# An attention and MLP kernel under another order table, with 38 products of zeros at its start and its flag behind the last result

## The chip, the cores and the metric

The kernel runs on one core of a Trainium2 chip. The metric is the device time of one execution in microseconds. TensorE (PE; PEld for its weight loads) multiplies, VectorE (DVE) and ScalarE (ACT) work element by element, GpSimd (POOL) does next to nothing here, and SyncE (SP) issues all DMAs, in one queue.

## The reference

Soft-capped attention over 4 batches of 12 heads (448 tokens, 64 columns a head), followed by a two-layer MLP with a sigmoid gate (768 to 2048 to 768). The MLP's weights arrive as 64-bit floats, and `q` and `k` are drawn some 5.8 times larger than 0.1 times a normal variable.

```python
scores = scale * np.matmul(q, k.transpose(0, 1, 3, 2))
scores = cap * np.tanh(scores / cap)
attn = np.exp(scores - np.max(scores, axis=-1, keepdims=True))
attn = attn / (np.sum(attn, axis=-1, keepdims=True) + 1e-09)
x = np.matmul(attn, v)                        # heads side by side: 1792 x 768
h = x @ w_in
out = (h * (1.0 / (1.0 + np.exp(-1.702 * h)))) @ w_out
```

## The kernel before

Heads are handled in pairs: 4 batches of 6 pairs make 24 units. A unit loads `q`, `k` and `v`, multiplies scores into two double banks `s` in four groups (three of two blocks, one of a single block), takes a tanh from each into `t` and an exponential into `p` on ScalarE, sums the exponentials with products by ones into the bank `sm`, and multiplies them with `v` into the single bank `pa`. The first seven units do so in 32-bit floats, with tiles in the room of `wo`; the later ones split every operand into two 16-bit halves (`qh`, `ql`, `vh`, `vl`). Of most units ScalarE copies `sm` to `f` and `pa` to `pu`; the sums go by DMA through memory (`sd`, `rsum`), VectorE takes reciprocals (`rr`), two more DMAs spread them (`rd`, `rb`), and VectorE makes the two halves of `x`. Units 4 and 5 divide directly, without the DMAs.

The MLP's first product takes `x` of all six units of a batch, one after the other, into one of two banks `m`: for each unit a chunk of three products, high by high, high by low, low by high. The weights come in half pieces of 512 KB as pairs of 32-bit words (tiles `g` and `wo`), and VectorE decodes them with integer steps into `wi_h` and `wi_l`; two of the passes can stand on ScalarE instead. The last two batches share seven products in place of eight in banks `z`, with sums of weights made on VectorE.

Every operation is recorded first (`Plan.op`), with a model cost. A table in the source, `ORDER`, then gives the whole order: which operation comes when, on which engine where two could do it, and which buffer of a ring each tile takes. `timed` computes start times by the model's costs and lags, and `emit` writes the instructions in that order; each engine runs its own in order. `keep_busy` would add products of zeros where the model sees TensorE idle before the first `m`; neither kernel has one from it, only those written out ahead. Before the table's first operation VectorE fills constants (lines 411 to 423), ending with the zeros `wz`, and TensorE multiplies zeros 16 times (line 427).

At the end small operations (lines 1253 to 1270) judge whether the ranges allowed the fast path and write one number, `flag`. All engines read it (line 365) and branch (line 366) to the end or into `general_path`, a slower kernel for any input. In the traced run no line of `general_path` was executed.

Of the kernel before, what the change touches and what calls it, by code (L numbers as in the profile page):

```python
# [11 lines left out]
F16 = mybir.dt.float16  # L12
F32 = mybir.dt.float32
# [24 lines left out]
EV_ON = ("AV", "AV")  # L38
SPLIT_ON = "A"
# [12 lines left out]
READ_ACC = 0.083  # L52
PE_COL = 0.0004222
# [3 lines left out]
LAG = {"PE": 0.165, "ACT": 0.1, "DVE": 0.085, "SP": 2.6}  # L57
DMA_ISSUE, DMA_BW = 0.5, 0.36
# [15 lines left out]
    "wI-b@8<=EjnaQR=;GUae%9+}MbtZwSVoI2TW~xbO)|;y4wyR+_m^!9#V7tj@c9^<>BBokkr`cs%nR@1sNn~1^X=b=-6R2*kyZinbrk!bTMwoYIo@r~|n=xjj>0l0<v1X?EU>@j?W}F!nc;tGTUM8{W80c;KnDJ(}"
    "x$g#=zGgz8lNn@YnSN%u8EyKT&Vd1Dc3_41VY--=fsJO4S!m`5ewvBqp#PVdYc`pu=7=e3Hk+enfeA6cO%t=nJa%O7xV>hZd0}pvErIFgmRV)k9x$r|Vh`y>0ne^6&jLOZ#~w6(bK5L7Ndj?gQgh5~HFwPEz`np4"
    "bH%(2+%*9c&pvQh&3&`q6brmE8Et&~z<e?Z>{)ZoB)8AqLzlunHwo?aKuVj%K5@lOD*MpfFpX_4``H9dZu`Q0F?sAc^TeDt$ITK0_N99iIAOk<ljdvSlzD7kxx6-O@Pc{mirA+vG|<F;Gs-5i+7`7-1I`w+iS1k0"
    ")S@-PX7-)S6dY{A*=44=jT}s3qgZQO*w^Nw$!C)W2ia^kwSD7S+Gj4AEpF4;^7fO9YSY^AHnY8FN?5;57mQ$A*@*VD%Wosu^tN?ylr3O0*a|izINC<Dg>7^@#uf}#v_4zXR<fn+SX<d%3beIl?H5<YmJW`yZEOr1"
    "2$r**Y$4m(z6n&dU)^}y&X%#?To?P^0k*e&><1ULU2R|6&Av6Yf<tVFU~L=IX1Cp~!qc{+t!8`J33iI@X{+0zcA~9e`&o^3Y)$*!eRRX@N;}Z*u>FIp>}As{xYG`>!-K2sNNaGHooaX6x^|i!Ve8p7c2e+!U2CTY"
    "Ev~aOt;0QbvR!XC+Z@3S_J`YRx7b<sknL^v**NaHJrkT^>)Y9Oqup;W+O2khJ!@~+h4zw-?{3<h_GIvujb%gaZHsu=zObk4w%|*<$TqNd>`%AdzOqN`YrDx_wr}il`_>)^-n9?yFE_{Dvk5}y+QpV|iG641+1U1I"
    "aK61}#a#&=vz}uN=ib{#HoRMEui6j62=1}9E*#zuKC^>^5uJ0-ZEE+xMsp2=EnIkv8~WRQvIlJ%_aqo*(Is`??MM5=rgap$%$~F9+*8}yC3ERrLYKiscb{!M7s-9GKW%as*=2R?Vz{sNn~i{tY#x`<#da}6tGFnk"  # L80
    "nOt5M%jI+V-7lNXMZ^N`w-t<p1zjpv(-m^HT#C@luCS}^vb&V7jyoR&*U{w&&E@L4mZ5E2Jr^0Px=t>OYwTj+R#(mCbUR#US0ps5^RSD{?Yg=Pwu$TQVq*2sZmy^+=9H`N!dw*W?uxsnE*3U$C0yyy9<EtvNms_z"
    "aHU)#7aIq-s2B&QyJ$GjHFwc*hKq}>+)P*24RL+kEEf+4xrU+fF~s$CjofUv+-?hP>*hG0o9p~;p4;HcxqwUT%Dcpv0Qb3}F6j2VexXTlnd|9>g|4s*-Tctu?tts>D!7gApgZJrXfL<OEq9@Afm`7gyCm+gONb|2"
    "QXK4-geJn3E*Z|oBW{&j>gM5UmmDj)5pIne=|;Ju?xY*-&bqWX#!U!Khnw6)H`c9n?c6wb%58V!-OkXFxY?Z!-Hf~3D4gWd;}+cFGT>+&i)Y+9w-r<1HXMiZaSWb!$J`#A>@wno&?#;bR&p0zAuNn3u?QB$y_gwG"
    "4Nir|mBxKI9#dl`oQ#!S8f+gr4X3&}gFCqWxBw>%K99TI6fA@5LbKphoQO*>D=x+LZaU7z6?g$xVh&t}*>Dvu$FexhmBa0r7oTA<%!!Y&IOfA#SORBYZY+s;up+L-nV22RV<o(Zvv3_=!aZ&W-oU+XC$7iJxO(tS"
    "JnpLCJzRtN@fPkHTos=TzKpwZ16Ic?SO9Nh1uTdM@F3p7LwFdEU=2Jm_$qG1lXw)X;Zr<@_ptyS$7_S@;7@#xZ}0(L#}8N&PvKj9IJhn@#25Gu3)4rui|_Ff*28r43DZ-3{EENuGd942VVS5Fe!<%K8*|e)JdK&D"
# [12 lines left out]
    "|GMSBccA}Mwf{m)4gdG6|999L?ZDW-<$~1?i8a!nvgc3D?~G#g=SQiKft@w%fc}IbD6+)H5nI&oS139(^arfL*}wA1(Vyv`lk>mAe*o)%ulf"
# [49 lines left out]
class Plan:  # L148
# [158 lines left out]
    def timed(self, pre, seqs):  # L307
# [6 lines left out]
        while any(at[e] < len(s) for e, s in seqs.items()):  # L314
            moved = False
            for e, s in seqs.items():
                while at[e] < len(s) and all(start[p] is not None for p, _ in pre[s[at[e]]]):
# [9 lines left out]
                    if e == "SP":  # L327
                        done[i] = pipe = max(pipe, t + us) + o.mb / DMA_BW
# [1114 lines left out]
```

## Time and profile before

| | us |
|---|---|
| runs without a profile, median of 3 (591.09 to 592.51) | 591.7 |
| the profiled execution | 594.05 |
| its span, first to last instruction | 591.9 |
| TensorE busy in the span | 577.8 |
| VectorE busy | 542.0 |
| ScalarE busy | 399.3 |

The profiled execution took 2.15 us more than its span, and 2.35 us more than the median of the runs without a profile. An engine's busy time says how much work it had, not whether anybody waited for it; for that there are the waits (who waited for whom, and how long) and the order of time. Units 0 to 6 end near 84 us; from there on the MLP's products fill TensorE.

### The profile page before, as it was taken

How to read it: one execution, taken by the hardware profiler on the slowest of the kernel's cores; microseconds unless marked ns; L12 is line 12 of the kernel's file. 1: busy time of each engine (PE TensorE's matmuls, PEld its weight loads, DVE VectorE, ACT ScalarE, POOL GpSimd, SP SyncE). 2: the span in 40 equal slices, each digit the busy share in tenths (PEclk: the TensorE clock that was granted, in tenths of full speed). 3: DMA queues.
4: the chain of work that ended last, by engine and by line, in shares of the span. 5: the costliest groups of instructions: out<-in, count | busy, mean ns of one | idle time of the engine just before them, and what ended most of it. 6: DMA issues, size and time to landing. Idle time of an engine off the chain costs nothing.

```text
span 591.9 us, 9836 instructions
## 1 busy us (share of the span) xinstructions
PE 577.8 (98%) x3674; PEld 288.5 (49%) x3674; DVE 542.0 (92%) x904; ACT 399.3 (67%) x617; POOL 0.2 (0%) x4
## 2 busy tenths in 40 slices
PE   7998899999999999999999999999999999999995
PEld 3333345555555554544555555555555555555552
DVE  4998999999999999999999999988999999988932
ACT  5998899989789899898787687434445543421110
POOL 0000000000000000000000000000000000000000
PEclk9999999999999999999999999999999999999999
DMA  8999763624567544343433444312222210000201
GB/s 298 328 239 294 227 239 108 205 71 139 157 172 209 193 141 141 95 137 110 148 86 101 120 153 133 104 48 81 88 71 82 64 45 0 17 0 1 79 31 69
DMA packets 45559, 74.36 MB, mean 126 GB/s; under 512 B 14952, under 2 KB 30912, under 8 KB 45504
## 3 DMA queue, kind: packets, MB, share of 16 engines
q1 hardware_dynamic: 45504, 73.66, 40.2%
q8 instruction: 31, 0.51, 0.3%
q14 instruction: 24, 0.20, 0.1%
HBM read 61.68 MB, written 11.95 MB: 124 GB/s over the span
## 4 chain that ended last, share of the span: by engine, by line
PE 73%; DVE 15%; DMA 5%; issue 3%; ACT 1%; SPq 1%; DVEq 0%
PE m L257 39%; PE z L257 22%; PE s L257 5%; PE pa L257 5%; DVE wo L222 3%; DVE p L222 2%; DMA sd<-f 2%; PE sm L257 2%; DMA g<-in_moe_w_in_dram 1%; DMA rb<-rd 1%; DVE g L222 1%; DVE rb L222 1%; DVE ta L222 1%; DVE ql L222 1%; DVE wi_l L222 1%
## 5 line engine op out<-in xcount | busy, mean ns | idle before, releaser
L257 PE MATMUL m<-g,wo 128*128 128x448 f16 x624 | 126.4, 353 | 0.0
L257 PEld LDWEIGHTS <-wo 128*128 128x128 f16 x864 | 83.4, 98 | 80.5 <-issue 3.6
L214 ACT ACTIVATE t<-s 128x896 f32<-128x896 f32 (+1 forms) x96 | 77.5, 823 | 22.9 <-DVE p L222 12.8
L257 PEld LDWEIGHTS <-wi_h 128*128 128x128 f16 x528 | 50.5, 98 | 53.1 <-issue 7.6
L257 PE MATMUL m<-x,wi_h 128*128 128x448 f16 x234 | 63.6, 353 | 1.4 <-DVE x L222 0.7
L222 DVE TENSOR_TENSOR p<-t,p 128x896 f16<-128x896 f32 (+1 forms) x62 | 58.5, 951 | 0.7 <-ACT p L238 0.4
L257 PE MATMUL m<-xa,wi_h 128*128 128x448 f16 x198 | 53.7, 353 | 0.0
L214 ACT ACTIVATE t<-t 128x896 f32<-128x896 f32 (+1 forms) x62 | 51.9, 846 | 0.6
L238 ACT ACTIVATE p<-t 128x896 f16<-128x896 f32 (+1 forms) x54 | 45.1, 841 | 3.3 <-PE pa L257 3.0
L257 PE MATMUL s<-qh,kk 128*128 128x448 f16 (+3 forms) x152 | 46.0, 377 | 0.0
L222 DVE SCALAR_TENSOR_TENSOR wo<-wo 128x1024 int32<-128x1024 int32 (+2 forms) x42 | 44.3, 1065 | 0.2 <-ACT wo L238 0.2
L257 PE MATMUL s<-ql,kk 128*128 128x448 f16 (+1 forms) x136 | 42.0, 353 | 0.0
L257 PE MATMUL m<-x,wi_l 128*128 128x448 f16 x117 | 41.2, 353 | 0.0
L257 PEld LDWEIGHTS <-stg 128*128 128x128 f16 x288 | 28.2, 98 | 26.3
L257 PEld LDWEIGHTS <-wi_l 128*128 128x128 f16 x264 | 25.8, 98 | 25.0 <-issue 1.0
L257 PE MATMUL pa<-p,vh 128*64 128x448 f16 x272 | 37.5, 355 | 0.2 <-DVE rb L222 0.2
L257 PE MATMUL m<-xa,wi_l 128*128 128x448 f16 x99 | 34.9, 353 | 0.0
L257 PEld LDWEIGHTS <-kk 128*128 128x128 f16 (+1 forms) x272 | 23.3, 101 | 22.5 <-issue 2.7
L257 PEld LDWEIGHTS <-xa 128*128 128x128 f16 x216 | 21.0, 98 | 19.6
L238 ACT ACTIVATE xa<-x 128x1024 f16<-128x1024 f32 x9 | 9.4, 1055 | 30.1 <-PE z L257 15.0
L257 PE MATMUL s<-wo 64*128 64x448 f32 (+1 forms) x96 | 24.7, 622 | 3.4 <-DMA wo<-in_q_dram 1.8
L257 PE MATMUL sm<-p,ones 128*32 128x224 f16 (+2 forms) x544 | 26.5, 306 | 0.0
(278 smaller groups left out, 1092.8 us busy)
## 6 DMA issues: line engine op xcount, KB each, us to landing
wo<-in_moe_w_in_dram SPq DMA_DIRECT2D x18, 512.0 KB, 5.4
stg<-in_kx_dram SPq DMA_DIRECT2D x17, 448.0 KB, 4.3
stg<-in_qx_dram SPq DMA_DIRECT2D x17, 448.0 KB, 3.8
stg<-in_moe_w_out_dram SPq DMA_DIRECT2D x16, 384.0 KB, 5.8
wo<-in_moe_w_out_dram SPq DMA_DIRECT2D x16, 384.0 KB, 8.4
sum<-xa SPq DMA_DIRECT2D x32, 192.0 KB, 3.7
stg<-sum SPq DMA_DIRECT2D x32, 192.0 KB, 2.9
rb<-rd SPq DMA_DIRECT2D x44, 112.0 KB, 3.2
```

What stands on the lines that cost most here:

```text
L214: self.nc.scalar.activation(real(out), real(in_), func, scale=real(scale), **b)
L222: getattr(self.nc.vector, name)(out=real(out), **{k: real(x) for k, x in ins.items()}, **kw, **a)
L238: self.nc.scalar.activation(real(out), real(in_), AF.Copy, scale=1.0 if f is None else f, **b)
L257: self.nc.tensor.matmul(real(o), real(w), real(x), start=a, stop=z)
```

## The change

The table `ORDER` is another one, made with a larger lag of DMAs (2.9 in place of 2.6 us, and 0.5 us more before 80 us), of ScalarE and VectorE, and with a cost for VectorE's operations that begin in the upper half of the partitions. The zeros are filled first, TensorE multiplies 38 of them (zeros by zeros, no ones), and the flag is written behind the last result. `general_path` becomes two loops over 48 heads and over 64 parts of the MLP, with an own copy `vn` of `v`; before, it was a loop over 24 units, a decoding that was written out, and a loop over 4 batches.

```diff
-LAG = {"PE": 0.165, "ACT": 0.1, "DVE": 0.085, "SP": 2.6}
-DMA_ISSUE, DMA_BW = 0.5, 0.36
+LAG = {"PE": 0.165, "ACT": 0.109, "DVE": 0.087, "SP": 2.9}
+DMA_ISSUE, DMA_BW, DMA_EARLY = 0.5, 0.36, 0.5
+WARM = 38
+UPPER = 0.23
...
 ORDER = (
-    "c-p;p1F+{!vSpSMzqW1Lwr$(C-F^SKecQHe+qP}nHeY`;`(|f1Uc`%;c)L|~PE}-NMpd1tjHpxqU_gTf1Of;7z2p!LQiBI6AUX)7fou>LQbGjC1u-Bkq=J}`6e2=)U`PiAy-1K7VnG?m0g)jORDjqJ1<FDk$O{!A"
+    "c-p;}bFe4RlIXLP=&^0vwr$(CJ#)S|bH=u9+qP}nHg|sa?!LXT`yzJt#=cis`RUAz?5M7+%0F5G0D=Y!1_&HPgVc~5(m)Ex1rZ=3q=ak`2_i#UNCinDI(QHTazlEE3If@o0wjSLkO$&IOvnLcAQmvBgR&40@<K(("
...
+        if any(isinstance(x, Ref) and x._at(0).base_partition() for x in w + list(ins.values())):
+            us += UPPER
...
                         done[i] = pipe = max(pipe, t + us) + o.mb / DMA_BW
+                        done[i] += DMA_EARLY * (t < 80.0)
...
-        r = tc.nc.values_load(flag, min_val=0, max_val=1)
+        r = tc.nc.values_load(flag)
         with tc.If(r > 0):
-            general_path(tc, q, k, v, cap, w_in, w_out, out)
+            general_path(tc, q, k, vn, cap, w_in, w_out, out)
...
+    wz = sb.tile([P, 128], F16, name="wz")
+    nc.vector.memset(wz, 0.0)
     capt = sb.tile([P, 1], F32, name="capt")
...
-    wz = sb.tile([P, 128], F16, name="wz")
-    nc.vector.memset(wz, 0.0)
     ps_m = ring([P, 512], F32, "m", 2, ps)
     plan.zeros, plan.idle_bank = wz, ps_m
-    for _ in range(16):
-        nc.tensor.matmul(ps_m["tiles"][0][:32, :128], ones16[2], wz, start=True, stop=True)
+    for _ in range(WARM):
+        nc.tensor.matmul(ps_m["tiles"][0][:32, :128], wz[:, :32], wz, start=True, stop=True)
...
-        with tc.For_i(0, B * NP) as u:
+    with tc.tile_pool(name="g_att", bufs=1) as att, tc.For_i(0, N) as i:
...
-    with tc.tile_pool(name="g_mlp", bufs=1) as mlp, tc.For_i(0, B) as b:
+    with tc.tile_pool(name="g_mlp", bufs=1) as mlp, tc.For_i(0, NFC * B) as i:
...
+    host["vn"] = inputs["v"].reshape(B * H, S, D)
```

Three places of the order. The first is SP's queue where the last `k` and `q` of batch 0, those of unit 5, are loaded (`wo<-in_k`, `wo<-in_q`); `in_moe_w_in` are half pieces of `w_in`, `sd`, `rsum`, `rd` and `rb` the sums on their way through memory, `kk` belongs to unit 6. Before:

```order
L263 DMA sd_156<-f_146 4x224
L263 DMA wo<-in_k_dram 128x448
L263 DMA wo<-in_moe_w_in_dram 128x1024 x2
L263 DMA rsum<-sd_156 112x2x4
L263 DMA kk_130<-in_k_dram 128x448
L263 DMA wo<-in_q_dram 128x448
L263 DMA sd_157<-f_144 4x224
```

Now, in the same queue:

```order
L267 DMA wo<-in_moe_w_in_dram 128x1024 x2
L267 DMA wo<-in_k_dram 128x448
L267 DMA rsum<-sd_179 112x2x4
L267 DMA rd_180<-rr_176 112x2x4
L267 DMA wo<-in_q_dram 128x448 x2
L267 DMA wo<-in_k_dram 128x448
L267 DMA sd_178<-f_168 4x224
```

The last `q` stood behind 18 half pieces of `w_in`; it now stands behind 14, next to the `q` of unit 4.

The second place is TensorE between the first chunks of the MLP (`m<-x`, two banks) and the chunks of the next unit's `x`. `sm` and `pa` are those of units 4 and 5, `s<-qh,kk` the scores of unit 6. Before, from the second chunk's last product on:

```order
L257 MATMUL m_91<-x,wi_l 128x448
L257 MATMUL sm_160<-p_142,ones_2_74 64x448 x2
L257 MATMUL sm_160<-p_143,ones_0_72 64x448
L257 MATMUL sm_160<-p_143,ones_1_73 64x448
L257 MATMUL pa_161<-p_140,wo 64x448 x2
L257 MATMUL s_165<-wo 128x448 x2
L257 MATMUL pa_161<-p_141,wo 64x448 x2
L257 MATMUL pa_161<-p_142,wo 64x448 x2
L257 MATMUL sm_160<-p_139,ones_2_74 64x448 x2
L257 MATMUL pa_161<-p_143,wo 64x448 x2
L257 MATMUL s_165<-qh_132,kk_130 128x448 x2
L257 MATMUL s_166<-wo 64x448 x2
```

There the third chunk follows. Now, the rows just ahead of the third chunk:

```order
L261 MATMUL sm_182<-p_162,ones_2_76 64x448 x2
L261 MATMUL sm_182<-p_163,ones_2_76 64x448 x2
L261 MATMUL sm_182<-p_164,ones_0_74 64x448
L261 MATMUL sm_182<-p_164,ones_1_75 64x448
L261 MATMUL pa_183<-p_161,wo 64x448 x2
L261 MATMUL pa_183<-p_162,wo 64x448 x2
L261 MATMUL pa_183<-p_163,wo 64x448 x2
L261 MATMUL pa_183<-p_164,wo 64x448 x2
L261 MATMUL s_188<-qh_155,kk_152 64x448 x2
L261 MATMUL s_187<-qh_155,kk_152 128x448 x2
L261 LDWEIGHTS wi_h
L261 MATMUL m_90<-x,wi_h 128x448
```

All of unit 5's sums and products with `v` and all scores of unit 6 now come ahead of the third chunk; before, they came behind the fifth, except for one group of unit 6's scores and one of unit 5's sums.

The third place is VectorE's end: `z` and `m` are banks with the last products, `cnt` and `flag` the verdict. Before:

```order
L1269 TENSOR_REDUCE cnt<-cnt 1x1
L222 SCALAR_TENSOR_TENSOR f_146<-m_90,stg_128 128x448
L1270 TENSOR_SCALAR flag<-cnt 1x1
L222 SCALAR_TENSOR_TENSOR rb_148<-m_91,stg_128 128x448
L222 SCALAR_TENSOR_TENSOR f_145<-z_4009,stg_129 128x448
L365 TENSOR_LOAD flag
```

Now:

```order
L1274 TENSOR_REDUCE cnt<-cnt 1x1
L224 SCALAR_TENSOR_TENSOR f_168<-m_90,stg_150 128x448
L224 SCALAR_TENSOR_TENSOR stg_148<-m_91,stg_150 128x448
L224 SCALAR_TENSOR_TENSOR rb_169<-m_91,rb_169 128x448
L224 SCALAR_TENSOR_TENSOR stg_149<-z_4018,rb_169 128x448
L1275 TENSOR_SCALAR flag<-cnt 1x1
L370 TENSOR_LOAD flag
```

The flag went from ahead of the last two results to behind the last one; SP's read of it went from between its stores to behind the last store.

## Rows read from the trace of the kernel before

**Rows 1.** The page's busy times: us, share of the span, instructions.

```profile
PE 577.8 (98%) x3674; PEld 288.5 (49%) x3674; DVE 542.0 (92%) x904; ACT 399.3 (67%) x617; POOL 0.2 (0%) x4
```

**Rows 2.** Stretches: us, busy of each engine (instructions), granted clock, DMA share, GB/s.

```profile
0.00:10.00 10.00, 6.75 (x30) 3.69 (x32) 1.76 (x22) 3.89 (x5) 0.20 (x4) 1.00 0.73 244
10.00:40.00 30.00, 29.65 (x230) 10.71 (x234) 29.38 (x39) 29.85 (x42) 0.00 (x0) 1.00 0.97 324
40.00:64.00 24.00, 20.12 (x106) 6.75 (x98) 20.18 (x27) 20.05 (x27) 0.00 (x0) 1.00 0.94 252
84.00:245.00 161.00, 160.80 (x1105) 83.24 (x1102) 158.83 (x268) 146.73 (x226) 0.00 (x0) 1.00 0.49 148
```

**Rows 3.** TensorE's waits: who waited for whom, us in total, times, longest.

```profile
PE s L257 <- DMA wo<-in_q_dram: 1.8, 1, 1.8
PE pa L257 <- ACT pu L238: 0.7, 1, 0.7
PE m L257 <- DVE x L222: 0.7, 1, 0.7
PE m L257 <- ACT x L238: 0.7, 1, 0.7
```

**Rows 4.** TensorE in order of time: start, us, operation, count [idle before <- releaser].

```profile
1.92 1.86 PE L427 MATMUL m<-wz,ones 128*32 128x128 f16 x16 [1.92 <-DVE thr L1253]
5.12 5.77 PE L257 MATMUL s<-wo 64*128 64x448 f32 x16 [1.34 <-DMA wo<-in_k_dram]
12.61 1.77 PE L257 MATMUL s<-wo 64*128 64x448 f32 x8
19.47 1.02 PE L257 MATMUL s<-wo 64*128 64x448 f32 x4
49.64 1.77 PE L257 MATMUL s<-wo 64*128 64x448 f32 x8 [1.75 <-DMA wo<-in_q_dram]
```

**Rows 5.** ScalarE in order of time, 7 to 21 us.

```profile
7.02 0.92 ACT L214 ACTIVATE t<-s 128x896 f32<-128x896 f32 x1 [4.78 <-PE s L257]
8.51 0.92 ACT L214 ACTIVATE t<-s 128x896 f32<-128x896 f32 x1 [0.58 <-PE s L257]
20.00 1.24 ACT L238 ACTIVATE wo<-wo 128x1024 f32<-128x1024 f32 x1
```

**Rows 6.** VectorE in order of time, 0 to 78 us.

```profile
0.82 0.06 DVE L411 MEMSET warm<- 128x1 f32 x1 [0.82 <-PEq L1416]
18.00 0.69 DVE L222 TENSOR_SCALAR wo<-wo 128x1024 int32<-128x1024 int32 x1
18.72 1.25 DVE L222 SCALAR_TENSOR_TENSOR wo<-wo 128x1024 int32<-128x1024 int32 x1
77.31 0.62 DVE L222 SCALAR_TENSOR_TENSOR x<-rb,x 128x448 f16<-128x448 f32 x1
```

**Rows 7.** VectorE's waits until 84 us: the row of w_in's pieces.

```profile
DVE wo L222 <- DMA wo<-in_moe_w_in_dram: 2.4, 2, 2.0
```

**Rows 8.** SP's queue in order of time, 27 to 43 us.

```profile
27.26 0.81 SPq L263 DMA_DIRECT2D wo<-in_moe_w_in_dram  x2
42.88 0.42 SPq L263 DMA_DIRECT2D wo<-in_q_dram  x1
```

**Rows 9.** The end in order of time: last result and last store.

```profile
585.65 0.62 DVE L222 SCALAR_TENSOR_TENSOR f<-z,stg 128x448 f32<-128x448 f32 x1 [1.07 <-PE z L257]
586.39 0.40 SPq L263 DMA_DIRECT2D out_dram<-f  x1
```

**Rows 10.** Lines 365 and 366: count, ns min/median/max, first and last start.

```profile
L365 PEldq TENSOR_LOAD <-flag x1: 488/488/488, 584.1 to 584.1; - x1
L366 SPq EVENT_SEMAPHORE  x8: 17/17/17, 587.4 to 590.6; - x8
L366 ACTq COMPARE_BRANCH  x1: 45/45/45, 584.4 to 584.4; - x1
L366 PEldq COMPARE_BRANCH  x1: 4227/4227/4227, 584.7 to 584.7; - x1
```

More of the change, by code (lines that the diff above doesn't have):

```diff
@@ L99 @@
+    "|9I>F8Cs(q82i^D8><}>YotFvJO-@$(<};^6l(idl6ID?Vzi13X>g<s8q0s)Lx(_4BmCt!{6qTl_{Zk_zv;gKl?<^8"
 )
@@ L357, in keep_busy, with tile_kernel @@
             self.nc.tensor.matmul(out[:cols, :128], z[:rows, :cols], z[:rows], start=True, stop=True)
-def tile_kernel(tc, q, k, qx, kx, v, cap, w_in, w_out, out):
+def tile_kernel(tc, q, k, qx, kx, v, vn, cap, w_in, w_out, out):
     with ExitStack() as outer:
@@ L1290, in general_path @@
     P = 128
-    NC = 7
-    NV = 8
+    N = B * NP * 2
+    QC = 112
+    NQ = S // QC
     NCC = DM // P
     NFC = DFF // P
-    QC = 112
-    NQ = S // QC
+    assert B == 4
+    M = DM * DFF // (N * P)
     drm = ctx.enter_context(tc.tile_pool(name="g_drm", bufs=1, space=bass.MemoryType.DRAM))
-    xt = drm.tile([B * NP, P, S], F32, name="xt")
-    md = drm.tile([2, S], F32, name="md")
+    xt = drm.tile([N, D, S], F32, name="xt")
+    md = drm.tile([1, S], F32, name="md")
+    wd = drm.tile([2, N, P, M], F32, name="wd")
     cst = ctx.enter_context(tc.tile_pool(name="g_cst", bufs=1))
-    ones = cst.tile([P, D], F32, name="ones")
-    nc.vector.memset(ones, 1.0)
     capt = cst.tile([P, 1], F32, name="capt")
@@ L1406 @@
-_INS = ["q", "k", "qx", "kx", "v", "cap", "moe_w_in", "moe_w_out"]
+    acc = cst.tile([P, B, NCC, S], F32, name="acc")
+    nc.vector.memset(acc, 0.0)
+    ps = ctx.enter_context(tc.tile_pool(name="g_ps", bufs=1, space=bass.MemoryType.PSUM))
+    qf, kf = (a.rearrange("b p (j d) s -> (b p j) d s", j=2) for a in (q, k))
+    bits = [w.bitcast(I32).rearrange("r n -> (r n)").rearrange("(i p m) -> i p m", p=P, m=2 * M) for w in (w_in, w_out)]
+    with tc.tile_pool(name="g_att", bufs=1) as att, tc.For_i(0, N) as i:
+        kd = att.tile([D, S], F32, name="kd")
+        qd = att.tile([D, S], F32, name="qd")
+        vo = att.tile([QC, NQ, 2 * D], F32, name="vo")
+        st = att.tile([P, 2, M, 2], I32, name="st")
+        one = bass.ds(i, 1)
+        nc.sync.dma_start(kd, kf[one].rearrange("o r s -> (o r) s"))
+        nc.sync.dma_start(qd, qf[one].rearrange("o r s -> (o r) s"))
+        nc.sync.dma_start(vo[:, :, :D], v[one].rearrange("o (c p) d -> (o p) c d", p=QC))
+        nc.vector.memset(vo[:, :, D:], 1.0)
+        for w in range(2):
+            nc.sync.dma_start(st[:, w].rearrange("p m t -> p (m t)"), bits[w][one].rearrange("o p m -> (o p) m"))
+        af = att.tile([P, 2, M], F32, name="af")
+        a = af.bitcast(I32)
+        L, H = st[:, :, :, 0], st[:, :, :, 1]
+        nc.vector.tensor_single_scalar(out=a, in_=H, scalar=0x7FFFFFFF, op=ALU.bitwise_and)
+        nc.vector.tensor_scalar(out=af, in0=af, scalar1=2.0**-15, scalar2=122880.0, op0=ALU.max, op1=ALU.min)
+        nc.vector.tensor_scalar(out=a, in0=a, scalar1=0x38000000, scalar2=3, op0=ALU.bitwise_xor, op1=ALU.logical_shift_left)
+        nc.vector.tensor_single_scalar(out=a, in_=a, scalar=0x7FFFFFFF, op=ALU.bitwise_and)
+        nc.vector.scalar_tensor_tensor(out=a, in0=L, scalar=29, in1=a, op0=ALU.logical_shift_right, op1=ALU.bitwise_or)
+        nc.vector.scalar_tensor_tensor(out=a, in0=H, scalar=-(2**31), in1=a, op0=ALU.bitwise_and, op1=ALU.bitwise_or)
+        nc.sync.dma_start(wd[:, one].rearrange("w o p m -> (o p) w m"), af)
+        qk = ps.tile([P, NCC, 512], F32, tag="s", name="qk")
+        for c in range(NQ):
+            nc.tensor.matmul(qk[:QC, c, :S], qd[:, c * QC:(c + 1) * QC], kd, start=True, stop=True)
+        mx = att.tile([QC, NQ], F32, name="mx")
+        nc.vector.tensor_reduce(out=mx, in_=qk[:QC, :NQ, :S], op=ALU.max, axis=AX.X)
+        nc.sync.dma_start(md.rearrange("o (c p) -> (o p) c", p=QC), mx)
+        mb = att.tile([QC, 1, S], F32, name="mb")
+        nc.sync.dma_start(mb[:, 0], md.to_broadcast([QC, S]))
+        nc.scalar.activation(mb, mb, AF.Tanh, scale=tsc[:QC])
+        kq = ps.tile([P, NCC, 512], F32, tag="s", name="kq")
+        for c in range(NQ):
+            nc.tensor.matmul(kq[:QC, c, :S], kd[:, c * QC:(c + 1) * QC], qd, start=True, stop=True)
+        t = att.tile([QC, NQ, S], F32, name="t")
+        nc.scalar.activation(t, kq[:QC, :NQ, :S], AF.Tanh, scale=tsc[:QC])
+        nc.vector.tensor_tensor(out=t, in0=t, in1=mb.to_broadcast([QC, NQ, S]), op=ALU.subtract)
+        nc.scalar.activation(t, t, AF.Exp, scale=capt[:QC])
+        pa = ps.tile([P, 512], F32, tag="pa", name="pa")
+        for c in range(NQ):
+            nc.tensor.matmul(pa[:, :S], vo[:, c], t[:, c], start=(c == 0), stop=(c == NQ - 1))
+        r = att.tile([D, S], F32, name="r")
+        nc.vector.tensor_scalar_add(r, pa[D:, :S], 1e-9)
+        nc.vector.reciprocal(out=r, in_=r)
+        nc.vector.tensor_tensor(out=r, in0=pa[:D, :S], in1=r, op=ALU.mult)
+        nc.sync.dma_start(xt[one].rearrange("o r s -> (o r) s"), r)
@@ new lines, in general_path @@
+    xv = xt.rearrange("(b c j) d s -> b (j d) c s", b=B, j=2)
+    wiv = wd[0].rearrange("i p m -> (i p m)").rearrange("(c p f n) -> f p c n", c=NCC, p=P, f=NFC)
+    wov = wd[1].rearrange("i p m -> (i p m)").rearrange("(f p n) -> f p n", f=NFC, p=P)
+    with tc.tile_pool(name="g_mlp", bufs=1) as mlp, tc.For_i(0, NFC * B) as i:
+        f = bass.ds(nc.s_assert_within(i >> 2, 0, NFC - 1, skip_runtime_bounds_check_because="i < 4 * NFC"), 1)
+        b = bass.ds(nc.s_assert_within(i & 3, 0, B - 1, skip_runtime_bounds_check_because="two bits"), 1)
+        x = mlp.tile([P, NCC, S], F32, name="x")
+        wi = mlp.tile([P, NCC, P], F32, name="wi")
+        wo = mlp.tile([P, DM], F32, name="wo")
+        nc.sync.dma_start(x, xv[b].rearrange("o p c s -> (o p) c s"))
+        nc.sync.dma_start(wi, wiv[f].rearrange("o p c n -> (o p) c n"))
+        nc.sync.dma_start(wo, wov[f].rearrange("o p n -> (o p) n"))
+        hp = ps.tile([P, 512], F32, tag="pa", name="hp")
+        for c in range(NCC):
+            nc.tensor.matmul(hp[:, :S], wi[:, c], x[:, c], start=(c == 0), stop=(c == NCC - 1))
+        e = mlp.tile([P, S], F32, name="e")
+        nc.scalar.activation(e, hp[:, :S], AF.Exp, scale=-1.702)
+        nc.vector.tensor_scalar_add(e, e, 1.0)
+        nc.vector.reciprocal(out=e, in_=e)
+        nc.vector.tensor_tensor(out=e, in0=hp[:, :S], in1=e, op=ALU.mult)
+        op = ps.tile([P, NCC, 512], F32, tag="s", name="op")
+        for d in range(NCC):
+            nc.tensor.matmul(op[:, d, :S], wo[:, d * P:(d + 1) * P], e, start=True, stop=True)
+        mine = acc[:, b].rearrange("p o c s -> p (o c) s")
+        nc.vector.tensor_tensor(out=mine, in0=mine, in1=op[:, :, :S], op=ALU.add)
@@ L1409 @@
+    for b in range(B):
+        nc.sync.dma_start(out.rearrange("(d p) (b s) -> b p d s", p=P, s=S)[b], acc[:, b])
+_INS = ["q", "k", "qx", "kx", "v", "vn", "cap", "moe_w_in", "moe_w_out"]
 def kernel(**inputs):
```

161 lines of the change are left out of this document (35 added, 126 removed).

## The prediction

> **What bounds the kernel now.** The busy shares come first [rows 1]: TensorE is busy for 577.8 of 591.9 us, VectorE for 542.0, ScalarE for 399.3. An order of instructions cannot take work from TensorE, only holes, so the second view is the stretches [rows 2]: between 40 and 64 us TensorE is busy for 20.12 of 24, later it is without holes (160.80 of 161 from 84 us). The third view says which holes count [rows 3]: one wait of 1.8 us for a q that was loaded late, 0.7 us for ScalarE to empty the bank of `pa`, and twice 0.7 us for x, all between 41 and 64 us. The last view is the start in order of time [rows 4, 5]: after 16 products of zeros TensorE idles 1.34 us until q and k of the first pair are there at 5.12, and its first 16 rows of `s` take 5.77 us, while 8 rows of the same kind take 1.77 us at 12.61. That is half the rate: zeros of 128 columns at one in 0.116 us on average, and `s` at 0.36 against 0.22 us a row, part of it waiting. The column of the granted clock reads 1.00 there [rows 2], so the lower of the two levels (1.2 against 2.4 GHz) is seen in the durations alone. Everything before 64 us that becomes earlier on TensorE can move the end; later there is next to nothing to win, but VectorE is nearly full from 84 to 245 us (158.83 of 161) and can take a lead back.
>
> **The general path** was not run: the flag was 0, and no row of the trace has one of its lines. Its new loops count only as code that the last branch jumps over (below). The two new planner terms and the lags count only through the table made with them.
>
> **Term 1, the start.** The memset of the zeros moves from last to first on VectorE, which begins at 0.82 [rows 6], so the products can start near 0.95 instead of 1.92. Thirty-eight at 1.86 / 16 = 0.116 us take 4.4 us at most and end at 5.4 at the latest, 0.3 us behind the landing at 5.12; the 1.86 us holds the last one's way through the array, so near 5.1 is likelier. TensorE then has no hole before the first `s`. Before, the first `s` was slow from 5.12 for some 4 us; with work since 0.95 the faster level should come near the first `s`. Upper bound of the gain: a block of four rows takes 1.02 us at the later rate [rows 4], so ScalarE's first tanh starts at 5.12 + 1.02 + 0.04 = 6.18 and not 7.02; the second block is ready at 5.12 + 1.77 = 6.89, its tanh follows the first at 7.02 instead of 8.51 [rows 5], and the exponentials start 1.5 us earlier. Lower bound: the level comes as late as before, or the zeros overrun, -0.3. I take 1.3 us of gain, near the upper end, since one block may still be slow. Between 10 and 40 us TensorE, VectorE and ScalarE are busy for 29.65, 29.38 and 29.85 of 30 us, so a lead at 10 us is kept if no engine gets more to do there. By the order, ScalarE has less: 10 instead of 14 decoding passes of 1024 columns (1.24 us each) up to the last exponential of the seventh pair. VectorE gets four of them at 0.69 us, but three integer steps of 1.25 us fall behind the last x of batch 0 [rows 6]: 2.8 - 3.8, so it reaches that x about 1 us of work sooner.
> By the Trainium skill (TensorE: Matmul & The Clock Gate, section Part 1: The HAM clock gate) the number of slow products at a kernel's start differs from run to run, as the moment of the rise is not tied to the first product. By it this term would be anything between its two bounds, and no run here yet shows which.
>
> **Term 2, the waits between 41 and 64 us.** They sum to 1.8 + 0.7 + 0.7 + 0.7 = 3.9 us [rows 3]. The q of the sixth pair was issued at 42.88 [rows 8], behind 18 half pieces of w_in, and the products that need it start at 49.64 [rows 4]. In the new order of SP's queue it stands behind 14; the 14th left at 27.26 to 28.1. Even if it goes five us after that, it lands before 41: the 1.8 us go. The second chunk of h waited twice 0.7 us for x of the second and third pair; in the new order all remaining products of the sixth pair and three `s` blocks of the seventh stand between the first chunk and the second: 1.4 us go. The 0.7 us behind `pu` stay: the bank is still single and `pu` still stands behind a decoding pass on ScalarE. What is late next: w_in's pieces, which give way to q and k on the queue, so waits of VectorE for w_in and of TensorE behind it. The nearest rows are VectorE's longest wait for w_in, 2.0 us [rows 7], and TensorE's own waits of 0.7 to 1.8 us. I put one new wait at 1.4 us, between these. Sum: -1.8 - 1.4 + 1.4 = -1.8 us; bounds -3.9 (all go, none comes) and +1.8 (none goes, one like the longest comes).
>
> **Term 3, from 64 to 585 us**: 0. Counts of each kind of work on each engine differ by a handful of passes, about +0.5 us on VectorE over the whole kernel, and TensorE's changes between kinds of products are 128 instead of 130. Bounds: 0 to +2.2, VectorE's idle time of 161 - 158.83 us, which is what it can still catch up if it comes late.
>
> **Term 4, the end.** Before, the flag was written ahead of the last two results; SP read it between the last stores, and TensorE at 584.1. Now every engine reads it behind the last result (before at 585.65 + 0.62 = 586.27 [rows 9]). SP loses the stop for the read between the stores, but the last store is gated by the last result anyway, at 586.39, and SP's waits for landings end at 590.6 [rows 10]. TensorE's read took 0.49 us and its branch 4.23, ScalarE's branch 0.05. If that stays, TensorE is through at 586.27 + 0.2 (an estimate for the flag) + 0.5 + 4.3 = 591.3, behind SP's last landing and ahead of the span's end at 591.9, which comes after SP's checks of all queues. I take +0.1; bounds -0.4 (stores less crowded) and +0.5.
> The Trainium skill (Runtime: NRT & Kernel Launch, section Instruction fetch mechanics) says that a taken branch to code outside what is held has to fetch it first. By that, the shorter general path would make TensorE's branch cheap and this term 0 or below; the 4.23 us agree that such a fetch exists.
>
> **Sum**: -1.3 - 1.8 + 0 + 0.1 = -3.0 us. The profiled execution took 594.05 us, 2.15 more than its span of 591.9; with the change such a one would take 591.05. The runs without a profile have a median of 591.7, 2.35 below the profiled one, and the same step gives 588.7 us.
>
> **Rivals.**
> Given back at VectorE: TensorE leads by 3 us at 64 us, but between 84 and 245 us VectorE is busy for 158.83 of 161 us, and TensorE runs into it. For: 2.2 idle us in 161 are little to catch up with. Against: VectorE's own waits before 64 us fall away too, 24 - 20.18 = 3.8 us in the stretch from 40. If only 0.5 us survive: 591.2.
> The clock comes no earlier, since TensorE's zeros use 32 of its columns: term 1 is 0, -1.8 + 0.1: 590.0. For: the 16 zeros of before did not bring it. Against: they were followed by 1.34 us of nothing.
> Everything goes: -1.5 - 3.9 - 0.4 = -5.8: 585.9. For: this is all that the waits hold. Against: static orders seldom lose all waits without a new one.
> Slower: VectorE starves for w_in. Four half pieces slip behind q and k, and if its waits for w_in grow from 2.4 to over 5 us, its work of 84 to 245 us starts late by more than the idle 2.2 us there, and TensorE waits for it: +2.2 us, 593.9. For: the 2.4 us [rows 7] are this very wait, and DMA is full there (share 0.94). Against: three integer steps of decoding were put off in the same order. It decides from the point at which VectorE's last x of batch 0 is later than 77.31 + 0.6 = 77.9 us, where it is now [rows 6].
>
> **Chances.** Forecast 0.48, with its own range 586.5 to 590.5 (term 1 from -0.6 to -1.5, term 2 from -0.7 to -3.3, the end from +0.1 to -0.4, rounded); given back 0.17; clock no earlier 0.08; everything goes 0.10; slower 0.17. About 0.2% (1.2 us) is what a measurement of this kernel can tell from no change. Faster: 0.48 + 0.10 + half of the clock's case, which lies 0.29% off, 0.04 = 0.62; within: 0.17 + 0.04 = 0.21; slower 0.17. The range goes from 585.0 to 593.5: it leaves out a half of the starved case and of the largest gain.
>
> **What would show it.** The first tanh at 6.2 to 6.6 and the second `s` block at the later rate (term 1); no wait of `s` for q, and fewer than 3 us of holes on TensorE between 41 and 64 (term 2); TensorE busy for 160 of 161 us in the stretch that answers to 84 to 245 (term 3); from TensorE's last product to the end of the span 6.3 us as now, and TensorE's branch as the only late engine (term 4). I am wrong if the tanh starts at 7 us, or if TensorE's lead at the end of batch 0 is there and is gone at 245 us, or if VectorE's waits for w_in grow.

## The result, and the profile after

The changed kernel takes 586.28 us (median of 4 runs, 585.83 to 587.47); the kernel before, run beside it, takes 592.11 us (591.09 to 592.58). The ratio is 0.9909, with an interval of 0.9893 to 0.9925: 5.8 us less by the medians, where 3.0 were forecast. The profiled execution took 586.16 us with a span of 584.1, against 594.05 and 591.9; that execution of before lay about 2 us above its median, so the spans differ by more than the medians do.

The busy times, as in [rows 1] (us, share of the span, instructions):

```profile
PE 577.9 (99%) x3696; PEld 289.4 (50%) x3696; DVE 542.1 (93%) x902; ACT 401.0 (69%) x619; POOL 0.2 (0%) x4
```

The work is the same to 0.1 us on TensorE and VectorE. The stretches, as in [rows 2] (busy of PE, PEld, DVE, ACT, POOL):

```profile
0.00:10.00 10.00, 8.72 (x56) 5.64 (x57) 3.07 (x19) 4.34 (x6) 0.20 (x4) 1.00 0.74 241
10.00:40.00 30.00, 30.00 (x240) 11.34 (x240) 29.75 (x44) 29.71 (x41) 0.00 (x0) 1.00 1.00 343
40.00:64.00 24.00, 23.12 (x116) 7.86 (x114) 23.96 (x30) 23.07 (x32) 0.00 (x0) 1.00 0.91 273
84.00:245.00 161.00, 161.00 (x1105) 82.93 (x1103) 158.69 (x267) 144.83 (x224) 0.00 (x0) 1.00 0.47 144
```

The third row is the one that moved: TensorE is busy for 23.12 of 24 us in place of 20.12, and VectorE for 23.96 in place of 20.18. TensorE's waits up to 90 us, as in [rows 3]:

```profile
PE m L432 <- DVE warm L418: 1.0, 1, 1.0
PE pa L261 <- ACT pu L242: 0.8, 1, 0.8
PE s L261 <- ACT t L216: 0.3, 1, 0.3
```

The waits for q and for x are gone, the one for `pu` is there as before. VectorE's wait of 2.4 us for pieces of `w_in` in `wo` [rows 7] has no row any more; for pieces in `g` it waits 3.7 us, all of it before 8.1 us. TensorE and then ScalarE in order of time, as in [rows 4, 5]:

```profile
1.00 4.24 PE L432 MATMUL m<-wz 128*32 128x128 f16 x38 [1.00 <-DVE warm L418]
5.26 2.57 PE L261 MATMUL s<-wo 64*128 64x448 f32 x8
8.09 1.92 PE L261 MATMUL s<-wo 64*64 64x448 f32 x8 [0.25 <-ACT t L216]
9.94 0.97 PE L261 MATMUL pa<-p,wo 128*64 128x448 f32 x4
```

```profile
7.12 1.73 ACT L216 ACTIVATE t<-s 128x896 f32<-128x896 f32 x2 [4.88 <-PE s L261]
```

The zeros end at 5.24 without a hole behind them, yet the first eight rows of `s` still take 2.57 us, against 1.77 at the later rate, and the first tanh starts at 7.12, not at 6.2 to 6.6. The second eight rows are at the later rate, and the first product of `pa` is at 9.94.

The end, VectorE's last result and SP's last store, as in [rows 9]:

```profile
580.09 0.62 DVE L224 SCALAR_TENSOR_TENSOR stg<-z,rb 128x448 f32<-128x448 f32 x1 [0.91 <-PE z L261]
```

```profile
580.74 0.33 SPq L267 DMA_DIRECT2D out_dram<-stg  x1
```

The last result begins 5.56 us earlier (585.65 - 580.09). From there to the end of the span it was 591.9 - 585.65 = 6.25 us and is now 584.1 - 580.09 = 4.0. In these last microseconds every engine reads the flag and branches, and SP waits until its stores have landed, as in [rows 10] (count, ns min/median/max, first and last start):

```profile
L371 SPq EVENT_SEMAPHORE  x8: 17/17/17, 582.2 to 582.8; - x8
L371 PEldq COMPARE_BRANCH  x1: 236/236/236, 581.4 to 581.4; - x1
L371 DVEq COMPARE_BRANCH  x1: 72/72/72, 581.4 to 581.4; - x1
L371 DVEq EVENT_SEMAPHORE  x1: 21/21/21, 582.0 to 582.0; - x1
```

TensorE's branch takes 0.24 us in place of 4.23. VectorE's, of 0.07 us, is followed by its next event after 0.6 us. In the kernel before that gap was 3.8 us, which the branch row alone does not show:

```profile
L366 DVEq COMPARE_BRANCH  x1: 72/72/72, 586.5 to 586.5; - x1
...
L366 DVEq EVENT_SEMAPHORE  x1: 21/21/21, 590.3 to 590.3; - x1
```

The last events of the kernel before are this one, at 590.3 us, and SP's, at 590.6 [rows 10], which wait for the last stores. Both are early now; which of them held the end cannot be read from these rows.

### The profile page after: what moved, and what is told of

The parts are those of the page before. It is cut to its first block, busy times and chain, and to the rows that moved or that the text cites. A ratio compares the mean times of both kernels' runs of the same rounds, so it can differ in the third digit from the quotient of the medians.

```text
span 584.1 us, 9864 instructions
## 1 busy us (share of the span) xinstructions
PE 577.9 (99%) x3696; PEld 289.4 (50%) x3696; DVE 542.1 (93%) x902; ACT 401.0 (69%) x619; POOL 0.2 (0%) x4
## 4 chain that ended last, share of the span: by engine, by line
PE 90%; DVE 6%; DMA 2%; ACT 1%; issue 1%; SPq 0%; ACTq 0%; DVEq 0%
PE m L261 48%; PE z L261 22%; PE s L261 9%; PE pa L261 8%; PE sm L261 3%; DVE wo L224 2%; DVE g L224 2%; DVE wi_l L224 1%; DMA g<-in_moe_w_in_dram 1%; DMA rb<-rd 1%; DVE wi_h L249 1%; SPq L267 0%; ACT p L216 0%; DVE g L249 0%; ACT wo L242 0%
## 5 line engine op out<-in xcount | busy, mean ns | idle before, releaser
L216 ACT ACTIVATE t<-s 128x896 f32<-128x896 f32 (+1 forms) x96 | 77.9, 821 | 17.1 <-PE s L261 8.5
L261 PE MATMUL pa<-p,vl 128*64 128x448 f16 x136 | 24.2, 352 | 0.0
```

Of the source, the lines that this page charges most:

```text
L216: self.nc.scalar.activation(real(out), real(in_), func, scale=real(scale), **b)
L261: self.nc.tensor.matmul(real(o), real(w), real(x), start=a, stop=z)
```

## The experiments

Theory: the table, the start and the general path each give a share, and the shares add up. Rivals: that one part carries the lead, or that a part works only with another. Each kernel ran beside the kernel before; ratios are against it, and intervals are in brackets.

**One part alone, and one part undone.** `table_only`, `start_only` and `general_only` put one of the diff's three parts into the kernel before. `no_general`, `no_start` and `no_table` are the changed kernel with one part as it was.

```diff
 # table_only: ORDER, LAG, DMA_EARLY, UPPER of the changed kernel
 # start_only
+    wz = sb.tile([P, 128], F16, name="wz")      # ahead of the constants
...
-    for _ in range(16):
+    for _ in range(38):
...
 # general_only: the new general_path, and
-        r = tc.nc.values_load(flag, min_val=0, max_val=1)
+        r = tc.nc.values_load(flag)
```

> The kernel before with the new order table alone (and the costs it was made with, and the flag behind the last result that comes with it); old start of 16 products, old general path. Theory A (the lead comes from the table's placing of work before 80 us, 4.7 us of the 5.6 us that TensorE leads by at its last product; the other 0.9 us come from the start): TensorE's last product ends 4.7 us earlier than before's; time -4.7 us, about 587.4, if the end costs what it cost before, and 588 to 589 if the branch of some 4 us now stands behind the last result and ends last. Rival B (the start is what carries the lead, by the clock, and the table fits only a kernel that started early): under 2 us of gain, 590.5 to 592.

> The kernel before with the new start alone (zeros filled first, 38 products of zeros); old table, old general path. Theory A: the later groups of the first scores are quicker, TensorE is ahead by 0.9 us at 10 us, but the old table's waits between 41 and 64 us for a late q and for w_in's pieces stand where DMA puts them, so at most 0.9 us reach the end: 591.2 to 592.1. Rival B: 3 us or more of gain, under 589.5.

> The kernel before with the new general path alone (not executed, since the flag is 0); old table, old start. Theory A (the time from TensorE's last product to the end of the span falls from 6.3 us, since the branch to the end takes a fraction of the 4.2 us on TensorE, and the last stores land without the stragglers seen at 588.5 to 590.3 us): 1 to 2 us of gain, 590.1 to 591.1, and TensorE's branch under 1 us. Rival B (the end is short in the changed kernel because its flag and its loads stand behind the last store; the general path plays no part): no change, 592.1, branch still about 4 us.

> The changed kernel with the old general path put back (not executed). Theory A: TensorE's branch takes about 4 us again and stands behind the flag, which is now behind the last result: from TensorE's last product to the span's end 6 us or more again in place of 4.05, time 587.5 to 588.5 (the changed kernel: 586.3). Rival B: 586.3, no change.

> The changed kernel with the old start (16 products of zeros behind VectorE's constants); new table, new general path. Theory A (parts add up): 1.5 us slower than the changed kernel, ratio to before 0.993 to 0.994. Rival B (the new table needs the early start, since its margins are made for it): 3 us or more slower, 0.996 or more. Rival C (the waits behind the start swallow it): as fast as the changed kernel.

> The kernel before with the new start and the new general path: the changed kernel without its order table. Theory A (the parts add up): 1.5 + 2.4 us less than before, ratio about 0.9935, and between 41 and 64 us TensorE waits again for 2 us or more in all, under whatever names. Rival B (the table's gain needs no start and general path, and these need no table; but the tail is counted twice): ratio 0.990 to 0.992, so that the table on top gives under 1 us.

`after_again` is the changed kernel once more.

> The changed kernel once more, on the same chip as the three beside it: a yardstick and a second trace. Both theories: ratio to before 0.989 to 0.993. Theory A (the three parts add up: -2.8 us table, -1.5 us start, and 1.1 to 2.4 us for the general path): 5.4 to 6.7 us less than before. Its first tanh at 6.3 or at 7.1 us, as the traced runs with the new start had it both ways.

| kernel | ratio to before | us less, of 593 |
|---|---|---|
| table_only | 0.9952 [0.9939, 0.9965] | 2.8 |
| start_only | 0.9975 [0.9962, 0.9988] | 1.5 |
| general_only | 0.9960 [0.9947, 0.9973] | 2.4 |
| no_table | 0.9937 [0.9918, 0.9957] | 3.7 |
| no_start | 0.9908 [0.9881, 0.9936] | 5.5 |
| no_general | 0.9928 [0.9915, 0.9941] | 4.3 |
| after_again | 0.9895 [0.9862, 0.9928] | 6.2 |

Every part gives something by itself. Table and start make 2.8 + 1.5 = 4.3 us, exactly what `no_general` measured; all three make 6.7, where the whole measured 5.4 (ratio 0.9909) and 6.2. The intervals are as wide as that difference, so the parts add up as far as these runs can tell. `no_start` is a mixed case: its median is 588.1 against 586.4 us for `after_again` on the same chip, 1.7 us, but the two intervals overlap. The expectation for `table_only` had 4.7 us from the table and was too high. Those for `start_only` (at most 0.9 us) and `general_only` (1 to 2 us) were low by the medians, though both intervals reach into them. `no_general` has TensorE's branch at 4.09 us again, and `no_table` has TensorE's waits again, as expected.

**The general path, written twice.** Nothing but the code that the branch skips grows.

```diff
             general_path(tc, q, k, vn, cap, w_in, w_out, out)
+            general_path(tc, q, k, vn, cap, w_in, w_out, out)
```

> The changed kernel with its new general path written out twice behind the branch (not executed). Theory A (the branch costs by how far it leads, that is by the instructions it skips): TensorE's branch, 0.24 us in the changed kernel, takes more than 1 us and up to the 4.1 us seen with the old path; up to 2.3 us slower than the changed kernel. Rival B (something that only the old path or its bounds on the flag held makes the branch slow): the branch stays at 0.24 us, same time as the changed kernel within 0.6 us.

Measured: 0.9943 [0.9922, 0.9964], median 589.5 us against 586.4 for `after_again` beside it: 3.1 us slower, by code that is never executed. First line 371 of `no_general`, then that of `general_twice`:

```profile
L371 PEldq COMPARE_BRANCH  x1: 4086/4086/4086, 581.7 to 581.7; - x1
L371 DVEq COMPARE_BRANCH  x1: 72/72/72, 581.8 to 581.8; - x1
...
L371 DVEq EVENT_SEMAPHORE  x1: 21/21/21, 584.7 to 584.7; - x1
L371 PEldq EVENT_SEMAPHORE  x1: 51/51/51, 585.9 to 585.9; - x1
```

```profile
L371 SPq EVENT_SEMAPHORE  x8: 17/17/17, 585.9 to 586.4; - x8
...
L371 PEldq COMPARE_BRANCH  x1: 442/442/442, 581.8 to 581.8; - x1
L371 DVEq COMPARE_BRANCH  x1: 72/72/72, 581.8 to 581.8; - x1
...
L371 SPq COMPARE_BRANCH  x1: 50/50/50, 582.1 to 582.1; - x1
L371 PEldq EVENT_SEMAPHORE  x1: 51/51/51, 582.3 to 582.3; - x1
L371 DVEq EVENT_SEMAPHORE  x1: 21/21/21, 585.7 to 585.7; - x1
```

The rows to compare are the branch and the next event of the same engine. With the old path TensorE goes on at 585.9 and VectorE at 584.7, and the span ends at 586.8. With the new path twice it is VectorE (585.7) and SP (585.9) that go on 3.9 and 3.8 us behind their branches, and TensorE does not; so the time came, and more of it than the theory's 2.3 us, but on other engines than it named. As the code is written, loop control not counted, the old path has 224 products on TensorE and 210 operations on VectorE, the new one 24 and 19, twice the new one 48 and 38. TensorE skipped 48 in 0.44 us where VectorE took 3.9 us over 38: the count alone does not decide it. The Trainium skill (Runtime: NRT & Kernel Launch, section Instruction fetch mechanics) says that a taken branch stalls when its target isn't among the instructions held, until they are fetched. The pairs of rows agree, and so do the fetches of instructions, which the trace lists among the DMAs by their queues, q8 and q14 (count, MB, share of the DMA engines' time). From 578 us on, first `no_general`, then the changed kernel:

```profile
q8 instruction: 2, 0.03, 1.2%
q14 instruction: 5, 0.04, 1.1%
```

```profile
q14 instruction: 3, 0.02, 0.6%
```

From 581.4 us on it is 7 to 9 fetches in the four traces with the old path, 7 with the new path twice, and 3 in each of the other nine. Where the borders of what is held lie, no run here shows.

From the start of VectorE's last result to the end of the span (called the tail) it is 4.0 us in all seven traces with new table and new path, 4.5 (`general_only`) and 4.8 (`no_table`) with the old table and the new path, 6.1 to 6.4 in the four traces with the old path, and 7.3 with the new path twice. So the short path is worth 1.3 to 2.4 us of the tail, and the new table another 0.5 to 0.8 us, but only with the short path (`table_only`, with the old one, has 6.4). This second share is not the place of the flag's read: in `general_only` too SP reads it behind its last store (586.1 and 585.68 us). But there SP's events behind the stores go on for 3.2 us from the start of the last result (to 588.2), against 2.7 in the changed kernel. The last four stores go out within 1.7 us there and within 2.6 us in the changed kernel; that the crowding makes them land late is likely, and was not tried.

With the new table the cause is plain: in `no_general` SP's events end at 583.4 and TensorE's branch is last, in `general_twice` VectorE and SP are. With the old table it is less so. `general_only` drops the bounds from the flag's read as well, and SP's read goes from ahead of its last four stores (584.1) to behind them, so the branch, the read and the landing of the stores move together. A kernel that drops the bounds alone was not run.

**What the start does.** `zeros16` keeps the zeros early but makes 16 of them; `wide_zeros` makes 38 with 128 columns of weights.

```diff
 # zeros16
-WARM = 38
+WARM = 16
 # wide_zeros
-        nc.tensor.matmul(ps_m["tiles"][0][:32, :128], wz[:, :32], wz, start=True, stop=True)
+        nc.tensor.matmul(ps_m["tiles"][0][:, :128], wz, wz, start=True, stop=True)
```

> The changed kernel with 16 early products of zeros in place of 38. Theory A (the gap between the zeros and the first scores, some 2.3 us here, lets the scores start slow as in the kernel before): first product of pa at 10.6 us in place of 9.9, time +1.6 us as without the new start. Rival B (only the earlier fill of the constants counts): as the changed kernel within 0.5 us.

> The changed kernel with the 38 zeros multiplied in 128 columns of weights in place of 32. Theory A (the moment at which the rate rises varies from run to run and the width plays no part): first tanh at 6.3 or 7.1 us, time equal to the changed kernel's within 0.6 us. Rival B (32 columns are too little to bring the higher rate, as the second rival of the prediction has it): first tanh at 6.3 us or before, and about 0.9 us faster than the changed kernel.

`zeros16`: 0.9923 [0.9895, 0.9951], median 588.1, like `no_start`; by the interval alone it is not told from the changed kernel, but its last result begins at 582.03 us, 1.9 us later. Its start:

```profile
1.00 1.89 PE L432 MATMUL m<-wz 128*32 128x128 f16 x16 [1.00 <-DVE warm L418]
5.24 6.30 PE L261 MATMUL s<-wo 64*128 64x448 f32 x16 [2.35 <-DMA wo<-in_k_dram]
```

The gap is back, sixteen rows take 6.30 us, the first product of `pa` is at 11.46 (expected at 10.6), and VectorE then waits for the first sums:

```profile
DVE f L245 <- PE sm L261: 1.1, 1, 1.1
```

So to fill the zeros early brings nothing unless they last until the first scores. Whether the gap or the smaller number of zeros does the harm is not separated, since the 38 differ in both. `wide_zeros`: 0.9894 [0.9867, 0.9922], median 586.95, as fast as `after_again`: width gains nothing that can be told. Its first tanh is at 6.39. But it is at 6.26 to 6.31 in the traces of `no_general`, `general_twice` and `q_back`, whose start is word for word that of the changed kernel with 7.12. In `q_back`:

```profile
0.99 4.24 PE L434 MATMUL m<-wz 128*32 128x128 f16 x38 [0.99 <-DVE warm L420]
5.25 1.77 PE L261 MATMUL s<-wo 64*128 64x448 f32 x8
```

Eight rows in 1.77 us behind the same zeros: the moment at which the rate rises differs from execution to execution, as the Trainium skill says (TensorE: Matmul & The Clock Gate, section Part 1: The HAM clock gate). And it is worth nothing here: the last result begins at 580.02 to 580.46 in the four traces with the early tanh, and at 580.09 and 580.03 in the two of the changed kernel, with the tanh at 7.12.

**The waits between 41 and 64 us.** `q_back` moves one DMA, the q of unit 5, back in the queue; `sm_first` fills TensorE's wait for `pu` with products that are ready. Both change two lines where the table is read.

```diff
+        listed = list(struct.unpack(f"<{n}H", raw[:2 * n]))
+        listed.insert(149, listed.pop(113))       # sm_first: insert(169, pop(178))
-        for x in struct.unpack(f"<{n}H", raw[:2 * n]):
+        for x in listed:
```

> The changed kernel with one DMA moved: the q of unit 5, issued at 29.6 us in the changed kernel, goes back behind the next four half pieces of w_in, as in the kernel before, to about 38 us. Theory A (the place of q in the queue is what the old wait of 1.8 us came from, and what TensorE loses before 64 us it does not get back): a wait of the scores for that q of 2 to 5 us near 39 to 43 us, and the end later by at least 1.5 us of it, 588 to 591. Rival B (q's place does not matter; whoever is late there was held by the sums' way through memory): no wait for q, under 0.6 us of difference.

> The changed kernel with one step of TensorE moved: four products of sm (0.92 us, at 42.9 us) go ahead of the products of pa that wait 0.6 to 0.8 us for ScalarE's copy pu at 41.4 us. Theory A (the one wait left on TensorE is filled, and TensorE sets the end): 0.5 to 0.8 us faster than the changed kernel. Rival B (what follows waits for the products of pa, or the wait reappears at the next copy): no gain, or slower by up to 0.5 us.

`q_back`: 0.9904 [0.9879, 0.9928], not told from the changed kernel. Its q goes out at 38.97 and the scores that need it start at 44.87 without a wait:

```profile
38.97 0.33 SPq L267 DMA_DIRECT2D wo<-in_q_dram  x1
```

```profile
44.87 1.82 PE L261 MATMUL s<-wo 64*128 64x448 f32 x8
```

The expectation took these scores to be the ones at 39 us; they come later, and to go out nine us later in the queue cost nothing. `sm_first`: 0.9898 [0.9872, 0.9923], no gain (median 587.1; its last result begins at 580.62). The four sums now stand ahead of the `pa` group, which still waits 0.44 us for `pu` and starts 0.57 us later than in the changed kernel (41.36):

```profile
40.52 0.97 PE L261 MATMUL sm<-p,ones 128*64 128x448 f32 x4
41.93 3.23 PE L261 MATMUL pa<-p,wo 128*64 128x448 f32 x16 [0.44 <-ACT pu L242]
```

Nothing comes of it at the end. What TensorE's waits are worth, neither run settles: `q_back` has no wait for q, and `sm_first` leaves TensorE no less idle from 10 to 80 us (1.04 us, 0.88 in the changed kernel). `q_back` does show that the place of q in the queue is not by itself what the old wait came from; its q still goes out 3.9 us earlier than in the kernel before (42.88 [rows 8]). `no_table`, with the old table, has these waits up to 90 us:

```profile
PE s L257 <- DMA wo<-in_q_dram: 1.5, 1, 1.5
...
PE m L257 <- DVE x L222: 0.7, 1, 0.7
...
PE m L257 <- ACT x L238: 0.5, 1, 0.5
PE pa L257 <- ACT pu L238: 0.4, 1, 0.4
```

**What goes with the end.** Of every trace one view more: busy times from 10 to 80 us. First the kernel before, then the changed one, `table_only`, `q_back` and `zeros16` (third figure: TensorE, fifth: VectorE).

```profile
10.00:80.00 70.00, 65.67 (x424) 24.04 (x428) 65.46 (x81) 65.84 (x90) 0.00 (x0) 1.00 0.93 293
```

```profile
10.00:80.00 70.00, 69.12 (x461) 26.36 (x460) 69.71 (x94) 66.56 (x91) 0.00 (x0) 1.00 0.96 321
```

```profile
10.00:80.00 70.00, 66.67 (x430) 24.74 (x432) 66.94 (x89) 64.23 (x89) 0.00 (x0) 1.00 0.94 313
```

```profile
10.00:80.00 70.00, 68.42 (x457) 26.22 (x456) 69.51 (x94) 66.17 (x91) 0.00 (x0) 1.00 0.98 319
```

```profile
10.00:80.00 70.00, 68.63 (x454) 26.32 (x452) 67.84 (x90) 65.32 (x90) 0.00 (x0) 1.00 0.94 317
```

Idle time is 70 less these. For all fourteen traces:

| trace | VectorE idle 10 to 80 | TensorE idle 10 to 80 | last result begins |
|---|---|---|---|
| after_again | 0.17 | 0.81 | 580.03 |
| after | 0.29 | 0.88 | 580.09 |
| q_back | 0.49 | 1.58 | 580.02 |
| wide_zeros | 0.51 | 1.78 | 580.36 |
| no_general | 0.64 | 2.08 | 580.44 |
| general_twice | 0.84 | 1.83 | 580.46 |
| sm_first | 0.88 | 1.04 | 580.62 |
| no_start | 1.49 | 1.72 | 581.63 |
| zeros16 | 2.16 | 1.37 | 582.03 |
| start_only | 3.03 | 3.29 | 583.56 |
| table_only | 3.06 | 3.33 | 583.23 |
| no_table | 4.36 | 3.33 | 584.35 |
| before | 4.54 | 4.33 | 585.65 |
| general_only | 4.73 | 4.17 | 585.03 |

The last result is at 579.9 us plus VectorE's idle time, within -0.4 and +1.2 us. The last result less the idle time spreads over 1.6 us for VectorE and over 3.0 us for TensorE: `sm_first` has less of TensorE's than `q_back` (1.04 against 1.58 us) and ends 0.6 us later, as VectorE's has it. ScalarE's does not order them at all (3.26 us in `no_table`, 3.44 in the changed kernel). This suggests that VectorE, which decodes `w_in` and makes x, sets the pace up to 80 us and that the new table leaves it no time to lose. An earlier tanh would then bring nothing because TensorE waits longer behind it, and it does: 1.58 to 2.08 us in the four traces with the early tanh, 0.81 and 0.88 in the two of the changed kernel. But this is argued, not shown: it is a fit over single executions (those of `before` and `no_table` lay 2 us above their medians), and a kernel that changes VectorE's idle time alone was not run.

No kernel of these beats the changed one by more than the measurement can tell.

## Why the prediction was right, and which step failed

It was right in sign, and the time lies in its range, 2.4 us below the number and 0.2 us outside the forecast's own range (586.5 to 590.5). The step that failed is term 4.

**Term 1, the start, -1.3.** Size right: 1.5 us [0.7, 2.3] alone and 1.7 when taken away (with overlapping intervals). The condition that it named as its proof of failure, the tanh at 7 us, occurred, and the term stood all the same. So the gain is not the first tanh. In `zeros16` it is lost where VectorE's first sums wait for the scores behind that tanh; that this is all of it was not tried. The rival by which the zeros bring nothing falls by `start_only`.

**Term 2, the waits, -1.8.** The table gives 2.8 us [2.1, 3.6] alone and 1.7 to 2.5 on top of the other parts (0.9937 less 0.9909 or 0.9895), so the size was about right. The working was not. The new wait of 1.4 us that it set against the old ones did not come: of 3.9 us, 0.8 are left. (Its price was taken from VectorE's longest wait for `w_in`, 2.0 us; the longest is 4.3 us, for the first piece, in another row of the same view.) And the place of q in the queue, the reason for its largest part, can be given back without loss (`q_back`). TensorE's waits did go, but what follows the end most closely is VectorE's idle time, 20.18 of 24 us busy [rows 2] against 23.96 now. The row was there and was used only against a rival. The slower case, VectorE starved for `w_in`, is refuted: the wait that it started from is gone, and VectorE's last x of batch 0, which was to be later than 77.9 us, starts at 69.28.

**Term 3, 64 to 585 us, 0.** Right. TensorE is busy for 161.00 of 161 us, and the lead is not given back at VectorE.

**Term 4, the end, +0.1 (bounds -0.4 to +0.5).** It is -2.2 us between the two profiled spans, and 2.4 us [1.6, 3.1] in `general_only`. The prediction said that the new loops "count only as code that the last branch jumps over" and then priced that jump, and SP's waits for landings to 590.6, as they were: "If that stays". They depend on the skipped code. Its own sign, 6.3 us from TensorE's last product to the end, failed (4.05 us now). Two readings led there. The 4.23 us of TensorE's branch [rows 10] ended before SP's last landing, so it looked covered; VectorE's stall, 3.8 us from its branch to its next event at 590.3, has a branch row of 72 ns and was not looked for. And the rule of the Trainium skill on taken branches (Runtime: NRT & Kernel Launch, section Instruction fetch mechanics), which gave a cheap branch for the shorter path, was noted beside the sum and given no chance of its own; its outcome is the one that came: TensorE's branch takes 0.24 us. The 2.3 us missing there (2.2 + 0.1) are most of the 2.8 us between forecast and result (5.8 - 3.0).

The rival in which everything goes (585.9 us) came nearest by its number, but that is luck: the wait for `pu` did not go, and the end brought 2.2 us where it had 0.4.

## What to carry to other kernels

When several engines are nearly full in one stretch, add up the idle time of each over that stretch and see which one moves with the end, before waits of the engine that bounds the whole are priced; then test it by a kernel that changes that engine's idle time alone. For a branch at the end, read on each engine the time from the branch to its next event, not the branch's own duration. Code that never runs can cost time there: 2.4 us in `general_only`, 3.1 us in `general_twice`.

## What the runs showed of the hardware that was not expected

From a taken branch over code that is not run to the engine's next event it was 0.2 to 1.0 us or 3.0 to 4.3 us on TensorE, VectorE and SP, with nothing between in fourteen traces, and which engine had the long one changed with the skipped code. With the old table and path the last stores landed late as well: SP's events behind them go on to 590.6 us [rows 10], 4.2 us behind the last store, against 582.8, 2.1 us behind it, in the changed kernel. Whether the fetching of code held them up was not tried. TensorE's rate at the start rose at different moments in executions of the same instructions (the first eight rows took 2.57 us in one and 1.77 us in another).
